# Two of four output blocks computed transposed, in 512-column products, and a first tile transposed in finer steps

## Chip, cores and metric

One Trainium2 chip, one of its cores. The metric is the device time of one execution in microseconds (us), as a median over executions; the span on a profile page, of one execution, is some 1.2 us shorter. PE is TensorE, DVE is VectorE, ACT is ScalarE, POOL is GpSimd, SP is SyncE, whose queue issues nearly all DMAs here.

## What must be computed

```python
x  = A_x                                   # [1, 2048, 640], bf16
xn = layernorm(x)
q, k, v = split(xn @ wqkv)                 # 32 heads of 20
phi(t)  = [softmax(t @ w_phi), softmax(-t @ w_phi)]       # per head, 40 features
o   = phi(q) @ (phi(k)^T v) / (phi(q) . sum phi(k))       # linear attention
h   = silu(xn @ w1) * (xn @ w3)            # F = 1536
out = x + o @ wo + h @ w2                  # the last line is what is changed
```

The last line, for 2048 tokens and 640 output columns, contracts 640 (wo) plus 1536 (w2) rows: 17 chunks of 128. The kernel works in four blocks (0 to 3) of 512 tokens, each of four tiles of 128 tokens.

## The kernel before

All operations are recorded by helpers and ordered by a scheduler of the program, which runs while the program is built: several streams offer their next step, and the one that can start first by a table of costs is committed. Each engine then runs its list in order. The output of a tile, in the kernel before:

```python
def out_tile(t, k):
    b, ti = divmod(t, 4)
    if t + 2 < T:
        load_xres(t + 2)                   # residual rows of x, 160 KB, two tiles ahead
    chunks  = [(oT[:, i, t * 128:(t + 1) * 128], wo_s, i) for i in range(DC)]        # DC = 5
    chunks += [(hT[b][:, i, ti * 128:(ti + 1) * 128], w2_s, i) for i in range(FC)]   # FC = 12
    ...                                    # the last tile is split 512 + 128 columns
    for n, (l, w, i) in enumerate(chunks):
        for q in range(2):                 # 2 x 320 columns: 34 matmuls a tile
            mm(bank(k + q, 320), l, w[:, i, 320 * q:320 * q + 320], n == 0, n == len(chunks) - 1)
    r = xres[:, t % 4, :].rearrange("p (b c) -> p b c", c=320)
    tt("DVE", r, bank2(k, 320), r, ALU.add)                   # PSUM + residual
    finish.append(P.dma("SP", out_t[:, t, :], xres[:, t % 4, :]))
```

The activations are the stationary operand (128 tokens), the weights stream past in two halves of 320 columns. The opening, where the normalised tile 0 is transposed on TensorE, copied out of PSUM and used at once:

```python
def xn_transpose(t, k, c0=0, c1=DC):
    for dc in range(c0, c1):
        tr(PSb[...128 * dc...], x_tok[:, t, 128 * dc:128 * dc + 128])   # TensorE
    ...
    if t < 2: copy("ACT", o, src)
    else:     evac(o, src)                                              # ACT or DVE

def transposes():
    for c, c0, c1 in ((1, 0, 2), (2, 2, DC)):       # chunks 0-1, then 2-4
        while done["first"] < c: yield None
        yield lambda ...: (xn_transpose(0, banks(1), c0, c1), keep_warm(1, 4 - c))  # dummies
```

`keep_warm` are dummy matmuls on a tile of zeros, which keep TensorE active while it waits.

The softmax here doesn't subtract the row's maximum and nothing guards it: scores larger than these inputs give would overflow.

## Time and profile before

| | kernel before |
|---|---|
| median of three executions | 266.67 us (266.32 to 266.89) |
| span of the profiled one | 265.6 us |
| TensorE, share of the span shown busy | 98% |
| matmuls of the output, blocks 1 and 2 | 8 tiles x 34, 320 columns each |
| other engines | DVE 69%, ACT 40%, POOL 36% |

The lines are in the prediction. One caution for reading them: a busy share of matmuls counts overlapping latencies, so what bounds TensorE is read from the *spacing of starts*: the time from one group's first start to the next group's, divided by the number of matmuls between.

### The profile page before, as it was taken

How to read it: one execution, taken by the hardware profiler on the slowest of the kernel's cores; microseconds unless marked ns; L12 is line 12 of the kernel's file. 1: busy time of each engine (PE TensorE's matmuls, PEld its weight loads, DVE VectorE, ACT ScalarE, POOL GpSimd, SP SyncE). 2: the span in 40 equal slices, each digit the busy share in tenths (PEclk: the TensorE clock that was granted, in tenths of full speed). 3: DMA queues.
4: the chain of work that ended last, by engine and by line, in shares of the span. 5: the costliest groups of instructions: out<-in, count | busy, mean ns of one | idle time of the engine just before them, and what ended most of it. 6: DMA issues, size and time to landing. Idle time of an engine off the chain costs nothing.

```text
span 265.6 us, 4673 instructions
## 1 busy us (share of the span) xinstructions
PE 261.2 (98%) x1875; PEld 156.6 (59%) x1898; DVE 184.3 (69%) x314; ACT 105.6 (40%) x225; POOL 96.0 (36%) x107
## 2 busy tenths in 40 slices
PE   8999999999999999999999999999999999999997
PEld 4655545565556746556554666555565657777773
DVE  4568999999869597769779695869695871211112
ACT  5646988799563235143144504054424010000000
POOL 4311587989969030604306070304361300000000
PEclk9999999999999999999999999999999999999999
DMA  7996078823300794374441527231909162231211
GB/s 227 271 309 186 4 160 238 172 52 52 121 2 0 177 252 79 69 93 77 101 81 26 111 52 155 61 70 26 136 6 178 42 139 52 74 95 56 75 50 49
DMA packets 62742, 27.73 MB, mean 104 GB/s; under 512 B 49920, under 2 KB 62720, under 8 KB 62720
## 3 DMA queue, kind: packets, MB, share of 16 engines
q1 hardware_dynamic: 62576, 27.26, 45.1%
q8 instruction: 15, 0.25, 0.4%
q10 hardware_dynamic: 144, 0.16, 0.2%
q14 instruction: 7, 0.06, 0.1%
HBM read 12.81 MB, written 2.62 MB: 58 GB/s over the span
## 4 chain that ended last, share of the span: by engine, by line
PE 95%; DVE 3%; ACT 1%; issue 1%
PE PS L104 95%; DVE S L104 1%; ACT eqt L104 1%; DVE rS L104 0%; DVE o_tok L104 0%; DVE t L104 0%; DVE hT L104 0%; ACT th L104 0%; DVE g_s L104 0%; DVE xres L104 0%; DVE zero L104 0%; DVE warm L104 0%
## 5 line engine op out<-in xcount | busy, mean ns | idle before, releaser
L104 PE MATMUL PS<-xnT,w_s 128*128 128x512 bf16 x462 | 105.1, 379 | 1.1 <-issue 0.2
L104 PEld LDWEIGHTS PS<-xnT,w_s 128*128 128x128 bf16 x480 | 46.1, 98 | 50.4 <-DVE xnT L104 0.3
L104 POOL TENSOR_TENSOR eqt<-eqt,rS 128x600 bf16<-128x600 bf16 (+1 forms) x32 | 41.0, 1306 | 85.9 <-DVE rS L104 85.9
L104 ACT ACTIVATE th<-PS 128x512 f32<-128x512 f32 x48 | 28.6, 596 | 71.9 <-PE PS L104 71.8
L104 PE MATMUL PS<-w_s,hT 128*128 128x320 bf16 (+2 forms) x384 | 54.9, 299 | 0.0
L104 DVE SCALAR_TENSOR_TENSOR t<-th,PS 128x512 bf16<-128x512 f32 x48 | 32.3, 672 | 26.0 <-ACT th L104 26.0
L104 PEld LDWEIGHTS PS<-w_s,hT 128*128 128x128 bf16 x384 | 37.1, 98 | 15.1
L104 PE MATMUL PS<-WVK,xnT 128*128 128x512 bf16 (+3 forms) x256 | 45.2, 329 | 0.2
L104 POOL TENSOR_TENSOR ekt<-ekt,rS 128x640 bf16<-128x640 bf16 x32 | 39.9, 1278 | 7.0 <-DVE rS L104 6.9
L104 DVE TENSOR_TENSOR xres<-PS,xres 128x640 bf16<-128x640 f32 (+2 forms) x17 | 13.4, 786 | 37.9 <-PE PS L104 37.9
L104 PEld LDWEIGHTS PS<-WVK,xnT 128*128 128x128 bf16 x260 | 24.2, 98 | 19.9 <-ACT WVK L104 0.4
L104 ACT ACTIVATE eqt<-PS 128x240 bf16<-128x240 f32 (+1 forms) x96 | 27.2, 347 | 20.8 <-PE PS L104 20.3
L104 DVE SCALAR_TENSOR_TENSOR hT<-t,PS 128x512 bf16<-128x512 bf16 x48 | 33.0, 687 | 1.8 <-DVE t L104 0.2
L104 DVE TENSOR_REDUCE S<-ekt 128x64 f32<-128x1280 bf16 x16 | 23.3, 1455 | 2.7 <-ACT ekt L104 2.7
L104 PE MATMUL PS<-Wqp,xnT 128*128 128x360 bf16 (+1 forms) x160 | 24.3, 299 | 0.0
L104 PE MATMUL PS<-wo_s,oT 128*128 128x320 bf16 (+2 forms) x159 | 24.3, 298 | 0.1
L104 DVE TENSOR_REDUCE S<-eqt 128x66 f32<-128x1320 bf16 x16 | 24.1, 1507 | 0.0
L104 ACT ACTIVATE ekt<-PS 128x640 bf16<-128x640 f32 x32 | 22.3, 702 | 1.3 <-PE PS L104 0.8
L104 PEld LDWEIGHTS PS<-Wqp,xnT 128*128 128x128 bf16 x160 | 15.3, 98 | 7.8
L104 PEld LDWEIGHTS PS<-wo_s,oT 128*128 128x128 bf16 x160 | 15.2, 98 | 6.2
L104 DVE RECIPROCAL rS<-S 128x64 f32<-128x64 f32 (+1 forms) x32 | 17.9, 560 | 1.1
L104 DVE TENSOR_TENSOR o_tok<-PS,g_s 128x360 bf16<-128x360 f32 (+1 forms) x32 | 15.7, 491 | 1.1
(51 smaller groups left out, 127.1 us busy)
## 6 DMA issues: line engine op xcount, KB each, us to landing
w_s<-in_B_w_dram SPq DMA_DIRECT2D x6, 640.0 KB, 6.4
xres<-in_A_x_dram SPq DMA_DIRECT2D x16, 160.0 KB, 2.5
out_dram<-xres SPq DMA_DIRECT2D x15, 160.0 KB, 1.8
x_tok<-in_A_x_dram SPq DMA_DIRECT2D x3, 640.0 KB, 5.1
w_s<-in_B_w_dram SPq DMA_DIRECT2D x1, 1920.0 KB, 9.6
wo_s<-in_A_wo_dram SPq DMA_DIRECT2D x1, 800.0 KB, 5.5
WVK<-in_A_wqkv_dram SPq DMA_DIRECT2D x2, 320.0 KB, 3.9
x_tok<-in_A_x_dram SPq DMA_DIRECT2D x3, 160.0 KB, 3.4
```

Of the source, the lines that this page charges most:

```text
L104: o = _Op(eng, lambda: m(*args, **kw), r, w, cost)
```

## The change

The intent: for blocks 1 and 2 make the output transposed. A slice of 128 columns of wo and w2 is the stationary operand and 512 tokens stream past it, so that 17 matmuls of 512 columns do what 27.2 of 320 did. The residual must then be transposed too (a transposing DMA loads x so), and the sum is transposed back by DMA before it is stored. The finer opening shall start the first product sooner.

```diff
+    def load_xT(b):
+        P.dma("SP", xT[b][:], A_x[0, 512 * b:512 * b + 512, :], True)      # True: transposing
+    def out_chunk(b, dc, k):
+        sel = slice(128 * dc, 128 * dc + 128)
+        chunks = [(wo_s, oT[:, i, b * 512:(b + 1) * 512], i) for i in range(DC)]
+        chunks += [(w2_s, hT[b][:, i, :], i) for i in range(FC)]
+        for n, (w, r, i) in enumerate(chunks):
+            mm(bank(k), w[:, i, sel], r, n == 0, n == len(chunks) - 1)
+        r = xT[b][:, dc, :]
+        tt("DVE", r, bank(k), r, ALU.add)
+    def turn_back(b, dc):
+        P.dma("SP", ot[b][:, :, 128 * dc:128 * dc + 128], xT[b][:, dc, :], True)
+    def store(b):
+        finish.append(P.dma("SP", out_t[:, 4 * b:4 * b + 4, :], ot[b][:]))
... (outs() calls out_chunk for blocks 1 and 2; load_xT(1) after block 0, load_xT(2) once
...  12 query tiles are made; blocks 0 and 3 stay as they were)
-            copy("ACT", o, src)
+            copy("DVE" if t == 0 and c0 == 1 else "ACT", o, src, 2)
+        while done["t0"] < 2:                       # in norms(), before tile 2's statistics
+            yield None
-        for c, c0, c1 in ((1, 0, 2), (2, 2, DC)):
+        for c, c0, c1 in ((1, 0, 1), (1, 1, 2), (2, 2, DC)):
...
-            yield lambda ...: (xn_transpose(0, banks(1), c0, c1), keep_warm(1, 4 - c))
+            yield lambda ...: (xn_transpose(0, 4 + min(c0, 2), c0, c1), keep_warm(1, int(c0 == 1)))
+            done["t0"] = c1
+                    while lo == 2 and done["t"] < 2:    # attention(): chunks 2-4 of the first product
+                        yield None                      # after tile 1's transposes
```

A remark on names: the code counts tiles from 0; "the second tile" below is tile 1.

More of the change, by code (lines that the diff above doesn't have):

```diff
@@ L305, in bass_parallel_sum__linear_kernel_hedgehog__glu_gated_swiglu__prompt_kernel @@
     zero = new("zero", [128, 128], bf, RT + 2048)
-    xres = new("xres", [128, 4, D], bf)
+    RR = region(4 * D * 2)
+    xres = new("xres", [128, 4, D], bf, RR)
+    xT1 = new("xT1", [128, DC, 512], bf, RR)
     RX = region(20480)
@@ L315, in bass_parallel_sum__linear_kernel_hedgehog__glu_gated_swiglu__prompt_kernel @@
     EqT0 = new("EqT0", [128, QC, 512], bf, RKV)
+    xT2 = new("xT2", [128, DC, 512], bf, RKV)
+    xT = {1: xT1, 2: xT2}
     RH = region(24576)
@@ L326, in bass_parallel_sum__linear_kernel_hedgehog__glu_gated_swiglu__prompt_kernel @@
     hT = [hT0, hT1, hT2, hT3]
+    ot = {1: new("ot1", [128, 4, D], bf, RH + 12288), 2: new("ot2", [128, 4, D], bf, RX)}
     RV = region(21504)
@@ L682, in load_xres @@
         P.dma("SP", xres[:, t % 4, :], x_t[:, t, :])
+    def load_xT(b):
[12 more added lines that the diff above has]
+        finish.append(P.dma("SP", out_t[:, 4 * b:4 * b + 4, :], ot[b][:]))
     def out_tile(t, k):
         b, ti = divmod(t, 4)
-        if t + 2 < T:
+        if t + 2 < 4:
             load_xres(t + 2)
@@ L713, in banks @@
         return min(range(0, 9 - n), key=free_at)
-    done = dict.fromkeys(("w", "ln", "t", "f", "k", "v", "n", "kv", "p", "pn", "pt", "q", "o", "h", "m", "first"), 0)
+    done = dict.fromkeys(("w", "ln", "t", "f", "k", "v", "n", "kv", "p", "pn", "pt", "q", "o", "h", "m", "first", "t0"), 0)
+    done.update({("u", b): 0 for b in range(NB)})
     landed, pace, force = {}, [0], [False]
@@ L803, in transposes @@
     def transposes():
-        for c, c0, c1 in ((1, 0, 2), (2, 2, DC)):
+        for c, c0, c1 in ((1, 0, 1), (1, 1, 2), (2, 2, DC)):
             while done["first"] < c:
                 yield None
-            yield lambda c=c, c0=c0, c1=c1: (xn_transpose(0, banks(1), c0, c1), keep_warm(1, 4 - c))
+            yield lambda c=c, c0=c0, c1=c1: (xn_transpose(0, 4 + min(c0, 2), c0, c1),
+                                                   keep_warm(1, int(c0 == 1)))
+            done["t0"] = c1
         done["t"] = 1
@@ L890, in outs, with turns, late_loads @@
         for t in range(T):
-            while done["o"] <= t or done["h"] <= t // 4:
+            b = t // 4
+            if b in xT:
+                if t % 4 == 0:
+                    while done["o"] < t + 4 or done["h"] <= b:
+                        yield None
+                    for dc in range(DC):
+                        yield lambda b=b, dc=dc: out_chunk(b, dc, banks(1))
+                        done["u", b] = dc + 1
+                continue
+            while done["o"] <= t or done["h"] <= b:
                 yield None
             yield lambda t=t: out_tile(t, banks(2))
+            done["u", b] = t % 4 + 1
+    def turns():
+        while done["u", 0] < 4:
+            yield None
+        yield lambda: load_xT(1)
+        for b in xT:
+            for dc in range(DC):
+                while done["u", b] < DC:
+                    yield None
+                yield lambda b=b, dc=dc: turn_back(b, dc)
+            if b == 1:
+                yield lambda: P.dma("SP", xres[:], x_t[:, T - 4:T, :])
+            yield lambda b=b: store(b)
+    def late_loads():
+        while done["q"] < 12:
+            yield None
+        yield lambda: load_xT(2)
     def set_held(d):
@@ L899, in bass_parallel_sum__linear_kernel_hedgehog__glu_gated_swiglu__prompt_kernel @@
     streams = [norms(), transposes(), fold_k(), attention(), k_norms(), loads(), queries(), q_norms(),
-               q_transposes(), o_transposes(), mlps(), outs()]
+               q_transposes(), o_transposes(), mlps(), outs(), turns(), late_loads()]
     MLPS, ATTN = 10, 3
-    URGENT = {0: 4.0, 4: 4.0, 7: 4.0, 8: 4.0, 9: 4.0}
+    URGENT = {0: 4.0, 4: 4.0, 7: 4.0, 8: 4.0, 9: 4.0, 12: 8.0, 13: 4.0}
     n = len(streams)
```

## The prediction

> **What bounds the kernel now.** I read the page's busy shares first, then the waits, then the groups of matmuls by shape, then two stretches of the timeline (the opening and the end), and last the DMA issues. Busy shares, and the two waits that the view of waits gives for TensorE alone:
>
> ```profile
> PE 261.2 (98%) x1875; PEld 156.6 (59%) x1898; DVE 184.3 (69%) x314; ACT 105.6 (40%) x225; POOL 96.0 (36%) x107
> ...
> PE PS L104 <- DVE warm L104: 1.1, 1, 1.1
> PE PS L104 <- issue: 0.2, 1, 0.2
> ```
>
> TensorE waits 1.3 us in the whole run, all of it in the first 12 us. But "98% busy" is no proof of a full engine, because each matmul is shown with its latency (379 ns at 512 columns) and overlaps the next. So I took the spacing of starts instead. The groups by shape, and one output tile of the end (34 matmuls: 10 with wo, 24 with w2):
>
> ```profile
> L104 PE MATMUL PS<-xnT,w_s 128*128 128x512 bf16 x462 | 105.1, 379 | 1.1 <-issue 0.2
> L104 PE MATMUL PS<-w_s,hT 128*128 128x320 bf16 x360 | 51.3, 299 | 0.0
> L104 PE MATMUL PS<-wo_s,oT 128*128 128x320 bf16 x150 | 22.8, 299 | 0.0
> ...
> 227.94 3.42 PE L104 MATMUL PS<-w_s,hT 128*128 128x320 bf16 x24
> ...
> 231.20 1.52 PE L104 MATMUL PS<-wo_s,oT 128*128 128x320 bf16 x10
> 231.40 0.82 DVE L104 TENSOR_TENSOR xres<-PS,xres 128x640 bf16<-128x640 f32 x1 [3.79 <-PE PS L104]
> ...
> 232.56 3.42 PE L104 MATMUL PS<-w_s,hT 128*128 128x320 bf16 x24
> ```
>
> From 227.94 to 232.56 is one tile: 4.62 us for 34 matmuls, 135.9 ns each. 320 columns at 2.4 a ns are 133.3 ns, so 2.6 ns per matmul is not columns. The 512-column products give the same: nine matmuls start from 11.84, and the next group starts at 13.79 (opening, below), so 216.7 ns each against 213.3, or 3.4 with the rounding of two printed times. There is no third term: from 11.84 us to the last product TensorE runs at its column rate, and the gaps left in the list of starts are each 216 ns long, one missing record (1875 matmuls are recorded for 1898 weight loads). The kernel is bound by matmul columns, plus an opening of about 11.8 us and an end of about 2 us behind the last product.
>
> The opening, where the first transposed tile is made:
>
> ```profile
> 5.23 0.35 DVE L104 TENSOR_SCALAR x_tok<-x_tok,mv,rstd 128x256 bf16<-128x256 bf16 x1 [0.52 <-POOL rstd L104]
> 5.61 0.37 DVE L104 TENSOR_SCALAR x_tok<-x_tok,mv,rstd 128x384 bf16<-128x384 bf16 x1
> 5.63 0.39 PE L104 MATMUL PS<-ident,x_tok 128*128 128x128 bf16 x2
> 5.90 0.48 DVE L104 BATCH_NORM_STATS2 bst<-x_tok 128x6 f32<-128x320 bf16 x1
> 6.06 0.38 ACT L104 ACTIVATE xnT<-PS 128x256 bf16<-128x256 bf16 x1 [0.88 <-PE PS L104]
> 6.44 0.45 DVE L104 TENSOR_SCALAR x_tok<-x_tok,mv,rstd 128x640 bf16<-128x640 bf16 x1
> 6.58 0.71 PE L104 MATMUL PS<-WVK,xnT 128*128 128x320 bf16 x4
> 7.12 0.44 PE L104 MATMUL PS<-ident,x_tok 128*128 128x128 bf16 x5
> ...
> 11.84 2.11 PE L104 MATMUL PS<-xnT,w_s 128*128 128x512 bf16 x9 [0.17 <-issue]
> 13.79 0.43 PE L104 MATMUL PS<-WVK,xnT 128*128 128x320 bf16 x2
> ```
>
> The reader is to see two chains in step: TensorE needs the copy that ends at 6.44 to start its first product at 6.58, and soon after, at 7.12, the second tile, normalised by DVE until 6.89.
>
> **What the Trainium skill says.** "TensorE: Matmul & The Clock Gate", section "Wait — 56ns, not 53.3ns?", gives a fixed cost of about 2.5 ns per warm matmul beside its columns; the 2.6 ns above agree. Its section "What's actually happening" says the clock starts gated to half and is released after sustained activity of about 3.4 us; here the dummy products are 107 ns apart for 128 columns until about 6.4 us, the cold rate, and products thereafter run at full rate. "Perfetto Trace Analysis", section "Identifying the Most-Contended Engine", warns that matmul busy share is a poor measure; the 379 ns against 217 ns apart show it. "DMA: Bandwidth & Descriptors", section "DMA Transpose (X-bar)", allows the transpose only into SBUF, which is why the transposed result must land in a buffer before it is stored.
>
> **The change part by part.** *Products of blocks 1 and 2.* Before, four tiles of 34 matmuls of 320 columns: 136 matmuls, 43,520 columns a block. After, five slices of 17 matmuls of 512: 85 matmuls, the same 43,520 columns. Not one column is saved; 51 fixed costs are. For two blocks 102 x 2.6 ns = 0.27 us, all on TensorE's path. The build confirms the count: 1792 TensorE instructions for 1898, which is 102 and four dummy products. Weight loads fall too (98 ns each, under a product of 136 or 217 ns): hidden, worth nothing.
>
> *Residual additions.* Eight of 825 ns leave (6.6 us), ten of 693 ns come (6.9 us; the row for 512 columns has 693). DVE is at 69%; in the stretch from the first to the last attention product I count 104 us of DVE work in both kernels, beside 126 us of TensorE work before and 133 after. No new bound.
>
> *DMA.* Eight residual loads and eight stores leave; two transposing loads of x (640 KB each), ten transposes back of 128 KB, one load and two stores of 640 KB come. None lies on TensorE's path unless the issuing queue, which works in order, makes a later transpose late. The rows to size this by:
>
> ```profile
> 42.03 5.84 SPq L116 DMA_TRANSPOSE wqkT<-in_A_wqkv_dram  x1
> ...
> EqT<-eqt SPq DMA_TRANSPOSE x16, 3.6
> ```
>
> A transpose of 800 KB holds the queue 5.8 to 7.3 us; at 640 KB about 4.7 to 5.9. The second such load stands ahead of the transposed query features of tile 12. From the last product that frees its buffer to the product that needs tile 12, the order on TensorE has 40 products of 217 ns and 20 query products (about 2.9 us): 11.5 us. The queue needs about 5.9 + 3.6 = 9.5. For the first load I get some 16 us against 13 to 14. Tight, but covered.
>
> *The end.* The last residual load waits for the five transposes back of block 1, and block 2's five products (18.3 us) lie between; I see some 10 us to spare. The last tile is as before.
>
> *Opening.* Four dummies go (4 x 107 ns = 0.43 us of TensorE) and the first copy halves, so the first product can start about 0.2 us earlier, at 6.37. But the second copy goes to DVE, in front of the statistics and the second tile's normalisation. I estimate 0.22 us for it, from 0.29 us for 256 columns and 0.36 for 384. It can't start before about 6.06, when ACT could see the transposes. Then statistics to 6.68, normalisation 6.60 to 7.05, and the second tile's transposes at about 7.11: where they are now (7.12). TensorE gets there early and waits. From there the order is the same, so the gain is 0.0, plus or minus 0.1.
>
> Sum: 266.67 - 0.27 - 0.0 = 266.4 us.
>
> **The rivals.** *The queue stalls TensorE*: a transposing load of x lands late and a query tile is not transposed in time. For it: the margin of only 2 us, and landings of 8 to 11 us of the two such loads before. Against: the order was made with such a cost in it, and the kernel before shows no wait on a DMA in TensorE's list. It would make 267.5 to 269. *The opening gains as drawn*: if DVE's copy fits into the time in which it waited for the reciprocal root (6.38 to 6.44) or is shorter, up to 0.3 us more, 266.1. *The clock is released later*, as TensorE now idles where it had dummies: up to one more window of 3.4 us at half rate, some 1.7 us lost, 268. Against: the dense dummies up to 5.4 us stay. *The 512-column form is worth more than its fixed cost* (fewer waits on PSUM banks): no, there are no such waits to remove.
>
> **Range and chances.** The three runs before span 0.57 us, more than the gain, so one tuning state of the opening already covers it. The costs are on the upper side: 265.7 to 267.4. Two per cent is 5.3 us; no mechanism above reaches it. Faster by 2%: 0.01; within 2%: 0.97; slower: 0.02.
>
> **What would show it.** Right: the tile's period of 18.5 us for four tiles becomes five slices of about 3.68 us; no wait of TensorE on a DMA after 12 us; the second tile's transposes near 7.1 us and the first 512-column group near 11.84. Wrong: a hole in TensorE's starts before a product with the query features (the queue), starts 107 ns apart after 6.5 us (the clock), or the first 512-column group well before 11.7 (the opening was worth more).

## The result

| | before | after |
|---|---|---|
| median of six executions | 266.58 us (266.32 to 267.02) | 266.57 us (266.24 to 266.80) |
| span of the profiled one | 265.6 us | 265.3 us |
| TensorE instructions (weight loads recorded) | 1898 | 1792 |
| DMA packets, MB | 62742, 27.73 | 72069, 29.03 |

All six executions of the changed kernel were fast, with a granted clock of 1.0; those of the kernel before lie within 0.3% of each other. The ratio of after to before is 0.9996, 95% interval 0.9983 to 1.0009: the same. (Here and below a ratio is the mean time of one kernel's fast runs over that of the other's fast runs of the same rounds, so not quite the ratio of the medians.) The predicted 266.4 lies 0.17 below the median and the range holds it. The range (265.7 to 267.4) is some six times as wide as the gain, so that it held says little; the mechanism has to be tested in the traces.

Profile after: the busy line of the page, then the whole list of waits of TensorE (us in total, times, longest).

```profile
PE 259.9 (98%) x1764; PEld 145.5 (55%) x1792; DVE 183.9 (69%) x316; ACT 106.2 (40%) x226; POOL 95.9 (36%) x107
```

```profile
PE PS L104 <- DVE warm L104: 1.1, 1, 1.1
PE PS L104 <- DVE x_tok L104: 0.7, 1, 0.7
PE PS L104 <- issue: 0.2, 1, 0.2
```

There is no wait on a DMA. The new 0.7 us on `x_tok` is in the opening, where dummies ran before: idle time in place of useless work.

The new groups (busy us, mean ns | idle before), from the page:

```profile
L104 PE MATMUL PS<-hT,w_s 128*128 128x512 bf16 x115 | 27.3, 379 | 0.3
...
L104 DVE TENSOR_TENSOR xT<-PS,xT 128x512 bf16<-128x512 f32 x10 | 6.9, 689 | 22.0 <-PE PS L104 22.0
```

And a slice of block 2 on the timeline of TensorE after (start, duration, then the group):

```profile
226.44 1.24 PE L104 MATMUL PS<-oT,wo_s 128*128 128x512 bf16 x5
227.52 2.75 PE L104 MATMUL PS<-hT,w_s 128*128 128x512 bf16 x12
230.11 1.24 PE L104 MATMUL PS<-oT,wo_s 128*128 128x512 bf16 x5
```

From 226.44 to 230.11 are 17 matmuls in 3.67 us, 215.9 ns each: 512 columns at 2.4 a ns are 213.3, so 2.6 ns are left per matmul, as at 320 columns. Five slices take 18.35 us where four tiles took 4 x 4.62 = 18.48.

The opening after, in the same rows as the prediction shows of before:

```profile
5.27 0.35 DVE L104 TENSOR_SCALAR x_tok<-x_tok,mv,rstd 128x256 bf16<-128x256 bf16 x1 [0.51 <-POOL rstd L104]
...
5.94 0.28 ACT L104 ACTIVATE xnT<-PS 128x128 bf16<-128x128 bf16 x1 [0.71 <-PE PS L104]
6.00 0.23 DVE L104 COPY xnT<-PS 128x128 bf16<-128x128 bf16 x1
...
6.19 0.49 DVE L104 BATCH_NORM_STATS2 bst<-x_tok 128x6 f32<-128x320 bf16 x1
...
6.28 0.72 PE L104 MATMUL PS<-WVK,xnT 128*128 128x320 bf16 x4
...
6.60 0.43 DVE L104 TENSOR_SCALAR x_tok<-x_tok,mv,rstd 128x640 bf16<-128x640 bf16 x1
...
7.09 0.45 PE L104 MATMUL PS<-ident,x_tok 128*128 128x128 bf16 x5
...
11.83 2.11 PE L104 MATMUL PS<-xnT,w_s 128*128 128x512 bf16 x9 [0.17 <-issue]
```

The first product starts at 6.28 and no longer at 6.58, but the second tile's transposes still start at 7.09 (7.12 before): the time gained is waited away. The DVE copy stands in front of the statistics, as drawn.

A correction to the reading in the prediction: the group at 11.83 shows nine matmuls, in both kernels. None of the eleven later profiles has the wait of 0.17 us on "issue" ahead of it, and all eleven have ten in this group, as here, on the timeline of the kernel with the changed products and the old opening:

```profile
11.44 2.33 PE L104 MATMUL PS<-xnT,w_s 128*128 128x512 bf16 x10
```

So one record is missing at the front of the group, and it starts one spacing earlier: at 11.62 before and 11.61 after. The "hole" ahead of it is 0.12 us and not 0.34.

With that, a profile splits into three terms which have different causes, and I use them in all experiments: (a) from the start of the first normalisation (5.23 before) to the second tile's transposes; (b) from there to the first 512-column group; (c) the *stretch* from that group's start to the start of the last matmul. Behind it lie 2.1 us in both kernels. The terms are worked out from the start times of the traces in ns, so they can differ by 0.01 from differences of printed lines.

### The profile page after: what moved, and what is told of

It reads as the page before. It is cut to its first block, busy times and chain, and to the rows that moved or that the text cites. A ratio compares the mean times of both kernels' runs of the same rounds, so it can differ in the third digit from the quotient of the medians.

```text
span 265.3 us, 4446 instructions
## 1 busy us (share of the span) xinstructions
PE 259.9 (98%) x1764; PEld 145.5 (55%) x1792; DVE 183.9 (69%) x316; ACT 106.2 (40%) x226; POOL 95.9 (36%) x107
## 2 busy tenths in 40 slices
DMA packets 72069, 29.03 MB, mean 109 GB/s; under 512 B 60272, under 2 KB 72048, under 8 KB 72048
## 4 chain that ended last, share of the span: by engine, by line
PE 96%; DVE 1%; DMA 1%; issue 1%; POOL 0%
PE PS L104 96%; DMA x_tok<-in_A_x_dram 1%; DVE bst L104 1%; DVE x_tok L104 0%; POOL rstd L104 0%; DVE mv L104 0%; DVE xres L104 0%; DVE xnT L104 0%
## 5 line engine op out<-in xcount | busy, mean ns | idle before, releaser
L104 ACT ACTIVATE eqt<-PS 128x240 bf16<-128x240 f32 (+1 forms) x96 | 27.2, 348 | 25.9 <-PE PS L104 24.1
L104 PE MATMUL PS<-w_s,hT 128*128 128x320 bf16 (+2 forms) x192 | 27.5, 299 | 0.0
L104 PE MATMUL PS<-hT,w_s 128*128 128x512 bf16 x115 | 27.3, 379 | 0.3
L104 PEld LDWEIGHTS PS<-w_s,hT 128*128 128x128 bf16 x192 | 18.3, 98 | 7.8
L104 DVE TENSOR_TENSOR xT<-PS,xT 128x512 bf16<-128x512 f32 x10 | 6.9, 689 | 22.0 <-PE PS L104 22.0
L104 PEld LDWEIGHTS PS<-hT,w_s 128*128 128x128 bf16 x120 | 11.7, 98 | 14.2
L104 DVE TENSOR_TENSOR xres<-PS,xres 128x640 bf16<-128x640 f32 (+2 forms) x9 | 6.7, 744 | 17.1 <-PE PS L104 17.1
```

The costliest lines, as they stand in the source:

```text
L104: o = _Op(eng, lambda: m(*args, **kw), r, w, cost)
```

## The experiments

Times are medians; "ratio" is to the kernel before on the same chip in the same rounds. Terms (a), (b), (c) are of the one profiled execution, in us.

| run | time | ratio (95%) | (a) | (b) | (c) stretch |
|---|---|---|---|---|---|
| before | 266.58 | | 1.89 | 4.51 | 251.85 |
| after | 266.57 | 0.9996 (0.9983-1.0009) | 1.82 | 4.52 | 251.59 |
| products only | 266.40 | 0.9986 (0.9973-0.9998) | 1.72 | 4.56 | 251.60 |
| opening only | 266.81 | 0.9996 (0.9982-1.0010) | 2.05 | 4.50 | 251.86 |
| slices in 2 x 256 columns | 266.84 | 1.0001 (0.9988-1.0013) | 1.86 | 4.51 | 252.03 |
| slices in 4 x 128 columns | 267.64 | 1.0030 (1.0018-1.0043) | 1.88 | 4.51 | 252.88 |
| the same, mended | 267.71 | 1.0046 (1.0031-1.0061) | 1.88 | 4.50 | 252.88 |
| second copy on ACT | 267.68 | 1.0038 (1.0026-1.0050) | 1.72 | 4.70 | 252.78 |
| queue plus 1 transpose | 266.49 | 0.9990 (0.9978-1.0002) | 1.78 | 4.51 | 251.61 |
| queue plus 3 | 270.20 | 1.0130 (1.0103-1.0156) | 1.86 | 4.51 | 256.02 |
| three blocks | 266.36 | 0.9985 (0.9973-0.9998) | 1.72 | 4.51 | 251.48 |
| changed kernel again | 266.36 | 0.9991 (0.9978-1.0003) | 1.86 | 4.79 | 251.60 |
| three blocks again | 266.50 | 0.9993 (0.9980-1.0005) | 2.22 | 4.51 | 251.48 |

My theory (A): the only gain is the fixed cost of the matmuls that are no longer issued, and everything else is hidden. Rivals: the products gain something else, or the opening loses what the products gain (B); the weight loads pace the products (C); the queue is near its limit and takes something back (D).

### Each half of the change alone

Products only is the changed kernel with the old opening:

```diff
-            copy("DVE" if t == 0 and c0 == 1 else "ACT", o, src, 2)
+            copy("ACT", o, src)
-        for c, c0, c1 in ((1, 0, 1), (1, 1, 2), (2, 2, DC)):
+        for c, c0, c1 in ((1, 0, 2), (2, 2, DC)):
-            yield lambda ...: (xn_transpose(0, 4 + min(c0, 2), c0, c1), keep_warm(1, int(c0 == 1)))
+            yield lambda ...: (xn_transpose(0, banks(1), c0, c1), keep_warm(1, 4 - c))
... (and the two added waits taken out again)
```

> The changed kernel with its opening put back to that of the kernel before; only the transposed products of blocks 1 and 2 remain. Theory A (the gain is the fixed cost of 102 matmuls, 0.27 us, and the finer opening is worth nothing): the last product group ends 0.25 to 0.30 us earlier in the trace than in the kernel before, first 512-column group at 11.8 us as there, time 266.3 (ratio to before 0.999). Rival B (the changed kernel gains in its opening and loses as much in the middle, to transposes that come late): this kernel is slower than the one before by the loss, 0.2 us or more, and its trace shows holes in TensorE's starts before products with transposed queries.

Opening only is the kernel before with these same hunks put in.

> The kernel before with the finer opening alone; products as before. Theory A (the copy put on DVE pushes the second tile's normalisation back by as much as the first product comes forward): first product at 6.3 us for 6.6, second tile's transposes at 7.1 as before, first 512-column group at 11.8, time 266.6, ratio 1.000 within 0.001. Rival B (the opening gains): first 512-column group at 11.5 or earlier, time 266.3 or less.

Measured: both correct. The stretch is 251.60 with the new products under either opening, and 251.85 or 251.86 with the old ones under either opening. The products are worth 0.24 to 0.26 us and nothing of it comes from the opening. The opening alone leaves time (ratio 0.9996) and stretch where they were. The times were expected at 266.3 and 266.6 and came out at 266.40 and 266.81.

### How much a matmul costs beside its columns

The slice is cut into more matmuls of the same total columns:

```diff
-            mm(bank(k), w[:, i, sel], r, n == 0, n == len(chunks) - 1)
+            for q in (0, 256):                      # and (0, 128, 256, 384) in the second
+                mm(bank(k, 256, q), w[:, i, sel], r[:, q:q + 256], n == 0, n == len(chunks) - 1, True)
```

> The changed kernel with each 512-column product of blocks 1 and 2 made as two of 256 columns: the same columns, 170 matmuls and 170 weight loads more. Theory A (2.6 ns fixed per matmul, weight loads of 98 ns hidden): spacing 109.3 ns, one slice of 34 matmuls 3.71 us for 3.67, in all plus 0.44 us against the changed kernel, time about 267.0. Rival C (the length of a product matters beyond its fixed cost, because a weight load of 98 ns needs about that much product to hide in): spacing above 112 ns, plus 1 us or more.

> As before but four products of 128 columns: 510 matmuls and weight loads more than the changed kernel. Theory A (a fixed cost alone): spacing 55.9 ns, plus 510 x 2.6 = 1.3 us, time about 267.9. Rival C (a weight load of 98 ns is longer than a product of 53 ns and now sets the pace): spacing 98 ns, 680 x 42 ns = 28 us more, time about 295; something between if loads are pipelined among themselves. The opening's transposes, 56 ns apart with a load each, speak for A.

Measured: the stretch is 0.44 us longer with 170 matmuls more and 1.29 us longer with 510 more: 2.6 and 2.5 ns per matmul. The timeline with four times 128 columns:

```profile
230.73 1.28 PE L104 MATMUL PS<-oT,wo_s 128*128 128x128 bf16 x20
231.85 2.84 PE L104 MATMUL PS<-hT,w_s 128*128 128x128 bf16 x48
234.53 1.28 PE L104 MATMUL PS<-oT,wo_s 128*128 128x128 bf16 x20
```

and its row of weight loads in the groups:

```profile
L104 PEld LDWEIGHTS PS<-hT,w_s 128*128 128x128 bf16 x480 | 27.2, 98 | 0.0
```

68 matmuls take 3.80 us, 55.9 ns each, each with a weight load of its own whose shown duration is 98 ns. A load is shown as longer than the product that it goes with, and yet the stream is no slower than columns plus 2.6 ns: loads overlap and don't pace TensorE here. Rival C falls, even for products far shorter than those of either kernel.

Both results were wrong (relative error 0.14 and 0.17): each part set the start flag in the same PSUM bank. The Trainium skill, "PSUM — Partial Sum Buffer", section "The four PSUM rules", says that a starting matmul clears the marks of the whole 2 KiB bank, so that the next chunk overwrote the other parts in place of adding. I took the flag away from all parts but the first, in the 128-column form:

```diff
-                mm(bank(k, 128, q), ..., n == 0, n == len(chunks) - 1, True)
+                mm(bank(k, 128, q), ..., n == 0 and q == 0, n == len(chunks) - 1, True)
```

> The 128-column form once more with the result mended: only the first matmul of a bank clears it, which the two split forms had done for each part. Same instructions, so theory A expects the same time as before, 267.7, stretch 252.88, and a correct result.

The result was correct and the stretch the same, 252.88. The page's rule is what these runs show, and the flag costs no time.

### The second copy on ACT

```diff
-            copy("DVE" if t == 0 and c0 == 1 else "ACT", o, src, 2)
+            copy("ACT", o, src)
```

> The changed kernel with one edit: the second of the two single-slice copies of the first tile goes back from DVE to ACT. Theory A (the copy in front of DVE's statistics is what holds the second tile): from the start of the first 256-column normalisation to the start of the second tile's normalisation 1.21 us as in the kernel before, for 1.33 in the changed one; the second tile's transposes about 0.1 us earlier (1.70 us after that start for 1.82), and the first 512-column group too; time 0.1 us less, too little for the timed runs to show (266.4 to 266.5). Rival B (something else holds the second tile, its root on POOL or its load): 1.33 us stays.

In the opening this came as expected: the second tile's normalisation starts 1.21 us after the first one (1.33 after the change), and term (a) falls from 1.82 to 1.72. The time was a plain miss: 1.0 us *slower* than the kernel before, not slightly faster than the changed one. The view of waits of TensorE, and the timeline around 18 us, have a wait that no other kernel had:

```profile
PE PS L104 <- ACT WVK L104: 0.5, 1, 0.5
```

```profile
17.14 0.79 PE L104 MATMUL PS<-BDc,wqkT 128*128 128x140 bf16 x12
18.41 1.90 PE L104 MATMUL PS<-xnT,w_s 128*128 128x512 bf16 x8 [0.48 <-ACT WVK L104]
```

The copy moved ACT's planned times, and the program's scheduler chose another order from there on; TensorE then met holes of 0.64 us at 17.8, 0.27 at 64.7 and 0.24 at 65.9, together 1.15 of the 1.19 us by which the stretch grew. So this run measures the opening, and nothing else of the change: a one-line edit here is not a one-line difference in the program.

### How much room the queue has

The second transposing load of x stands in the queue ahead of a transpose of query features (`EqT`) that TensorE needs. After the change, the queue and the product:

```profile
187.02 3.37 SPq L116 DMA_TRANSPOSE xT<-in_A_x_dram  x1
190.43 1.34 SPq L116 DMA_TRANSPOSE EqT<-eqt  x1
```

```profile
198.35 0.47 PE L104 MATMUL PS<-KVc,EqT 128*128 128x63 bf16 x11
```

The load holds the queue 3.37 us; the `EqT` transpose issued at 190.43 lands 3.7 us later (the median of its row), at about 194.1, and is needed at 198.35: room of 4.2 us. (This is not the tightest place of the changed kernel. The `EqT` transpose of tile 7, issued at 154.0 just ahead of the *first* load of x, landed after 4.5 us, where the median is 3.7, and 0.5 us before its product. No experiment loads that place.) To test the room behind the second load, one or three more such loads go behind it, into memory that nobody uses then, and nearly free by the scheduler's table of costs:

```diff
-        yield lambda: load_xT(2)
+        def more():
+            load_xT(2)
+            for d in spare[:1]:                     # spare[:3] in the second
+                o = P.dma("SP", d[:], A_x[0, 1024:1536, :], True)
+                o.part, o.cost = False, 0
+        yield more
```

> The changed kernel with one useless transposing load of 640 KB more behind the second load of x, same order on TensorE. In the changed kernel the next transposed query tile lands at about 194.1 us and is needed at 198.35: 4.2 us of room. One load holds the queue 3.4 us. Theory A (transfers are hidden while the room lasts): no hole, the stretch from the first 512-column group to the last matmul stays within 0.1 us of the changed kernel's 251.6, time 266.5. Rival (any time on the issuing queue costs): up to 3.4 us more.

> The same with three useless loads: 10.2 us of queue for 4.2 us of room. Theory A: one hole of about 6 us in TensorE's starts before the first attention product of tile 12, and the stretch 5 to 6.5 us longer, time 271.5 to 273. If the rival that no transfer ever matters were true: 266.5.

Plus 1: the queue is held 2.93 us more and the stretch is 251.61, 0.01 longer: hidden. Plus 3: the time is 270.20. Its queue and TensorE:

```profile
190.20 9.12 SPq L116 DMA_TRANSPOSE sp<-in_A_x_dram  x3
199.37 1.45 SPq L116 DMA_TRANSPOSE EqT<-eqt  x1
```

```profile
196.11 4.48 PE L104 MATMUL PS<-xnT,w_s 128*128 128x512 bf16 x20
203.17 0.47 PE L104 MATMUL PS<-KVc,EqT 128*128 128x63 bf16 x11 [2.57 <-DMA EqT<-eqt]
203.48 2.32 PE L104 MATMUL PS<-Wqp,xnT 128*128 128x360 bf16 x10
205.60 2.16 PE L104 MATMUL PS<-oT,wo_s 128*128 128x512 bf16 x5
```

The hole is 2.74 us between starts (2.57 waited), where I expected some 6: the scheduler had put ten more 512-column products ahead of the product that waits, which raised its room to about 6.3 us. But the stretch grew by 4.42. The rest is the clock. Here is the table of stretches (width, busy time of PE, PEld, DVE, ACT, POOL, granted clock, DMA share, GB/s):

```profile
196.00:200.40 4.40, 4.40 (x23) 1.96 (x20) 4.33 (x5) 2.56 (x8) 2.37 (x2) 1.00 1.10 232
200.40:203.10 2.70, 0.19 (x1) 0.00 (x0) 2.06 (x4) 0.00 (x0) 2.70 (x3) 1.00 1.13 216
203.10:207.40 4.30, 4.23 (x26) 2.35 (x27) 2.06 (x5) 1.81 (x6) 0.02 (x1) 0.61 0.98 181
207.40:212.00 4.60, 4.60 (x32) 2.23 (x31) 2.99 (x6) 0.22 (x1) 2.57 (x2) 0.99 0.14 26
```

After the hole the granted clock is 0.61 on average for 4.3 us: asked for finer windows, the profile gives 1.00 up to 204.0, so for 0.8 us after TensorE went on, then 0.50 from 204.1 to 207.4. There matmuls of 512 columns start 427 ns apart, twice 213. That costs 4.42 - 2.74 = 1.68 us more. Of the six timed executions three (270.62 to 271.62) list a granted clock of 0.994 and three (268.98 to 269.79) of 1.0, about 1.7 us apart by their means: the same hole sometimes costs the clock and sometimes not. Theory D is right in its mechanism, and beyond the room of this change.

### The same change on a third block

Products only, with block 0 transposed too (its buffers in memory that is free by then; the last MLP block waits until block 0 is stored):

```diff
-    xT = {1: xT1, 2: xT2}
+    xT0 = new("xT0", [128, DC, 512], bf, RE)
+    xT = {0: xT0, 1: xT1, 2: xT2}
-        yield lambda: (load_xres(0), load_xres(1))
+        yield lambda: (load_xT(0), load_xT(1))
... (and ot0 at RE + 5120; MLP block 3 waits for store(0))
```

> The transposed products on blocks 0, 1 and 2 with the opening of the kernel before: 153 matmuls fewer than the kernel before instead of 102. Theory A (each matmul saved is 2.6 ns): stretch from the first 512-column group to the last matmul 0.40 us shorter than before (251.85), that is 251.45, and 0.13 us shorter than with two blocks; time 266.2, ratio 0.998. Rival: without block 0's products as early filling the attention stretch gets waits on DVE or on transposes, and the stretch is longer than 251.6.

Correct; the stretch is 0.37 us shorter than before and 0.125 shorter than with two blocks (products only): 153 and 51 matmuls fewer, 2.4 and 2.5 ns each. The expected waits did not come, though the first load of x, issued right behind the load of w2 (1920 KB), held the queue for 9.8 us (8.7 when run again) where such loads hold it 2.7 to 4.1 us elsewhere. The median, 266.36, was the lowest so far, so it was run once more beside the changed kernel, both unedited:

> The changed kernel unaltered, on one chip with the next two. Theory A: stretch from the first 512-column group to the last matmul 251.6 us as in its first trace, time within 0.1 us of 266.55, ratio to before 0.999 to 1.000. The opening depends on when the clock is released: with an early release the second tile's normalisation starts 1.33 us after the first, 0.12 later than with the old opening.

> Three blocks with the old opening again, beside the changed kernel. Theory A: 0.13 us less in the stretch (251.46) and about 0.1 us less in the opening: 0.2 to 0.25 us below the changed kernel, 266.3. If the timed difference is below 0.1 us, the finer opening costs nothing.

Changed 266.36 (ratio 0.9991), three blocks 266.50 (0.9993): the stretches repeat to 0.01 us (251.60 and 251.48), and the times don't follow them. By the rule (a timed difference below 0.1 us in favour of three blocks means that the finer opening costs nothing) the timed runs would clear the opening; but the five runs of three blocks alone span 0.63 us, so they can't decide it. The two profiled executions show what lies over them. First DVE in the opening of the changed kernel run again, then of three blocks run again:

```profile
8.01 0.49 DVE L104 BATCH_NORM_STATS2 bst<-x_tok 128x6 f32<-128x320 bf16 x1 [0.57 <-DMA x_tok<-in_A_x_dram]
```

```profile
6.42 0.49 DVE L104 BATCH_NORM_STATS2 bst<-x_tok 128x6 f32<-128x320 bf16 x1 [0.56 <-DMA x_tok<-in_A_x_dram]
...
6.83 0.43 DVE L104 TENSOR_SCALAR x_tok<-x_tok,mv,rstd 128x640 bf16<-128x640 bf16 x1
```

In each, the statistics of a later tile waited some 0.57 us for their load of x, and as they stand in DVE's list ahead of the normalisation that is ready, this came late too: term (a) is 2.22 in three blocks, term (b) 4.79 in the changed kernel, where 1.72 (old opening) and 4.51 are usual. So three blocks are the best by the trace, by 0.12 us, and no version is shown to beat the changed kernel in time.

## Why the prediction was right

**The bound and the gain.** Right, and its reason is shown: 102 matmuls fewer gave 0.24 to 0.26 us of stretch, and four other counts (170 and 510 more, 153 and 51 fewer) the same 2.4 to 2.6 ns each. The step was 102 x 2.6 = 0.27 us, so 0.01 to 0.03 too much. A gain of 0.1% is near what a timed comparison can see: the first one gave 0.01 us between medians. The six comparisons with transposed products and nothing that made the stretch longer (after, products only, queue plus 1, three blocks, and the last two again) have ratios of 0.9985 to 0.9996, on average 0.9990, that is 0.26 us; only two of the six intervals lie wholly below 1, and the six share four sets of runs of the kernel before, so they are not independent.

**Weight loads, DVE, end.** "Hidden, worth nothing" holds for the weight loads, shown by the 128-column products. DVE's ten additions took 689 ns each (I took 693), and no wait on them shows. The end was as drawn: 2.1 us behind the last product in both, and the last residual load landed at 239.6 us, 10 us before its first use (249.6). One count was wrong and cost nothing: twelve residual loads of 160 KB leave, not eight (16 before, 4 after), as block 3's four become the one of 640 KB.

**The queue.** The verdict was right (no wait on a DMA) and the sizes were not: the load of 640 KB holds the queue 3.4 us and not 4.7 to 5.9, and the room is 4.2 us and not 2. I had scaled from the weights' transposing load at 42 us. The cost that I gave the rival, 267.5 to 269, left out that a hole can bring back the half clock: with three more loads it became 270.2.

**The opening.** The steps hold to 0.1 us (first product 6.28 for 6.37, DVE copy 0.23 for 0.22, normalisation from 6.60, transposes 7.09 for 7.11). "Gain 0.0, plus or minus 0.1" holds too against the profile of before, term (a) 1.82 for 1.89. But that profile flattered the change. In the two other kernels with the old opening and no late load, (a) is 1.72, and so it is with the copy on ACT; the changed opening has 1.78 to 1.88, and 2.05 in one profile (opening only). The copy in DVE's list thus costs about 0.1 us. In the profile of before the clock was released only at 6.46 (in products only at 3.82, in three blocks at 4.10); its dummies and transposes ran 107 ns apart, its first product came late, and the four products ahead of the second tile's transposes filled TensorE until 7.12. Term (b) is 4.50 to 4.56 in eleven of thirteen profiles, under either opening: what the first product gains reaches nothing behind the second tile's transposes. When the clock is released late, no gain shows either: the changed opening with a release at about 6.7 (the mended 128-column form) has (a) = 1.88, and the old one with 6.46 (before) has 1.89. These are single profiles. The latest release (opening only, at 6.95) has (a) = 2.05 and no old opening at the same phase beside it.

**The clock rival.** It did not happen, but not for the reason given. The release came at 3.8 to 6.5 us in the profiles with the old opening (three blocks, unedited: 4.10 once and 6.54 once) and at 4.0 to 7.0 with the changed one, by the spacing of starts. It varies with the execution, and no effect of the dummies that were taken away shows; whether they had a part in the latest release, 6.95, one profile can't say.

## What to carry to other kernels

Where TensorE starts its matmuls without holes, changing the form of a product at the same number of columns was worth its count of matmuls times 2.5 ns and no more (here for 128 to 512 columns): compute that before building the transposes it needs. Hiding a transfer is a matter of room at one particular product, so measure the hold of the queue and the room rather than a share, and remember that a hole may cost more than its length (here 2.74 us, and then 1.68 us at half clock). In a program whose order is made by costs, check what else an edit has moved before reading its time, and compare terms of the trace that start and end at fixed instructions when the effect is smaller than the scatter of the first loads.

## What the Trainium skill lacked or had wrong

- "TensorE: Matmul & The Clock Gate", section "Back-to-back issue gap", gives some 81 ns (128 columns) and 131 ns (512) per matmul for a sustained stream of weight loads and matmuls, and calls N/2.4 + 2.5 the isolated gap only. Here, with a weight load for each matmul, the stream runs at 55.9 ns (128 columns), 135.9 (320) and 215.9 (512): the formula called isolated is what holds, and 131 ns for 512 columns was never seen (the shortest distance of two starts in the thirteen traces is 214 ns).
- The same page, section "Why this matters for your kernels", asks for no idle gap over about 3 us. Here a hole of 2.74 us (2.57 waited) was followed by half clock (512-column starts 427 ns apart, granted clock 0.50 from 204.1 to 207.4 us); by the listed clocks this came in three of six executions.
- The same page, section "Part 4: PE-mode transpose", says that the full clock does not engage for transposes. Here the five transposes of the second tile start 55 to 56 ns apart once the clock is released, the spacing of warm products of 128 columns. So transposes run at the full clock; whether they alone would release it, which may be what the page means, no run here shows.
- The same page, section "What you observe", puts the release at about 4 us of activity, give or take 0.5. Dummies start at 1.05 us here, and the release came at 3.8 to 7.0 us, so 2.8 to 5.9 us after, between executions of nearly the same opening.
- "DMA: Bandwidth & Descriptors", section "DMA Transpose (X-bar)", has no figure for how long a transposing DMA holds its issuing queue (the page's only such times stand in its part on trn3, in cycles and for other sizes). Here: 2.7 to 3.4 us for 640 KB from DRAM in the kernels with two blocks, but 9.8 and 8.7 us right behind the load of 1920 KB in those with three; mostly 1.2 to 1.3 us for the 128 KB transposes back, up to 2.6; 1.3 to 2.7 us for the query features.
